# One PSUM tile for the early pairs and the dense layer, two dense tiles begun early, and q/k transposed by DMA from group 9

## The chip, the cores and the metric

The kernel runs on one core of one Trainium2 chip. The metric is the device time in microseconds (us) of one execution; the lower the better. A profiled execution of each kernel gives a trace, from which all durations below are taken.

## What is computed

Attention at two scales feeds a dense layer. For q, k, v of shape 8 x 8 x 576 x 64 (batch, heads, positions, width) the reference does, in essence:

```python
q_d = q.reshape(B, H, Sd, 4, D).mean(axis=3)      # k_d, v_d likewise
out_up = np.repeat(sm_attn(q_d, k_d, v_d), 4, axis=2)
mask = np.abs(pos[:, None] - pos[None, :]) < 4
scores = np.where(mask, scale * q @ k.T, -1e9)     # local attention
x = out_up + softmax(scores) @ v                    # then (4608, 512)
h = x @ w_in                                        # (4608, 2048)
out = (h - np.tanh(h)) @ w_out                      # (4608, 512)
```

## The kernel before, in words

**Attention.** The work is cut into 32 pairs of heads, and two pairs form one of 16 groups. Per group, q and k are loaded (`load_qk`), sorted into bf16 (`reorder`, line 491), transposed so that the width lies on the partitions (`turn`: nine TensorE transposes into PSUM, line 520, and a copy out, line 529; from group FI on, a DMA transpose on the SyncE queue instead, line 511, and a copy from SBUF), and summed over four positions (lines 533, 538). Per pair, `attention` makes the scores (lines 587, 606), their exponentials on ScalarE (623, 649, 652), a mask on VectorE (627, 656), the products with v (669, 675), the normalisation on VectorE (686, 688), and a transposition back into `xT`: by TensorE for pairs under 12 (lines 723/728 with a copy at 734, or 744 to 748), by a DMA transpose for the others (`lnT`, line 698) with two VectorE adds (line 708).

**Dense layer.** `dense(kb)` runs over nine blocks of 512 positions. `mm1` (line 777) makes one of 16 tiles of h with four matmuls of 128 x 512; ScalarE takes the tanh out of PSUM into `u` (line 786); VectorE subtracts it from the same PSUM bank into `gT` (line 789). `mm2` (line 832) makes one of four output tiles from 16 such matmuls; ScalarE copies it to `y` (line 843), and a DMA stores it. The last output tile is cut in three (`last_tile`, line 807). From block 2 on, `mm1` of one block and `mm2` of the block before alternate, so one pass through four `mm1` tiles and one output tile is 32 matmuls.

**PSUM.** [...] `ps_ts` and `ps_ox` hold two each for the attention. The other four are first `ps_ts1` and `ps_ox1`, two two-bank tiles for pairs 0 and 2, and then, once a pool is closed and another opened (`dense_banks`), four tiles of one bank each, `ps_hy0` to `ps_hy3`, which the dense tiles take in turn.

**Order.** `Program` collects operations with their engine, an assumed cost, and the keys that they read and write; `order` lays them out in time by priority, and `emit` issues every engine's instructions in that order. Where several engines may do an operation, tables (`RE`, `TU`, `TS`, `AS`, `AD`, `CV`, `UP`, `VD`, `RS`) say which. `spare` adds slack behind an operation before its user may be laid. `filler` puts matmuls on `warm` into idle places of TensorE until the first dense tile. The keys of `Program` decide the order alone. [...]

Of the kernel before, what the change touches and what calls it, by code (L numbers as in the profile page):

```python
# [8 lines left out]
FP32 = mybir.dt.float32  # L9
BF16 = mybir.dt.bfloat16  # L10
AF = mybir.ActivationFunctionType
ALU = mybir.AluOpType
PSUM = bass.MemoryType.PSUM


class Program:
# [20 lines left out]
    def op(self, eng, ns, fn, reads=(), writes=(), pri=0):  # L37
        i = len(self.ops)
        deps = set()
        for key in reads:  # L40
            if key in self.last_write:
                deps.add(self.last_write[key])
        for key in writes:
            if key in self.last_write:
                deps.add(self.last_write[key])
            deps.update(self.readers.get(key, ()))
        for key in reads:
            self.readers.setdefault(key, set()).add(i)
        for key in writes:
            self.last_write[key] = i  # L50
            self.readers[key] = set()
        deps.discard(i)
        self.ops.append((eng, ns, fn, deps, pri))
        self.touch.append(set(reads) | set(writes))
        return i
# [108 lines left out]
def kernel(  # L164
# [26 lines left out]
    N_DC = Dm // 128  # L191
# [4 lines left out]
    psum = ctx.enter_context(tc.tile_pool(name="psum", bufs=1, space=PSUM))  # L196

    def fixed(name, shape, dt, n=None, pool=const):
        if n is None:
            return pool.tile(shape, dt, name=name, tag=name)  # L200
        return [pool.tile(shape, dt, name=f"{name}{i}", tag=f"{name}{i}")
                for i in range(n)]
# [17 lines left out]
    vd = fixed("vd", [128, 2, 4, 65], BF16, NVW)  # L220
# [7 lines left out]
    lnT = fixed("lnT", [128, 7, 128], BF16, NLN)  # L228
    od = fixed("od", [128, G], BF16, 2)
# [6 lines left out]

    ps_ts = fixed("ps_ts", [128, 2, 512], FP32, pool=psum)
    ps_ox = fixed("ps_ox", [128, 2, 512], FP32, pool=psum)
    ps_hy = []


    early = ExitStack()
    psum_e = early.enter_context(tc.tile_pool(name="psum_e", bufs=1, space=PSUM))
    ps_ts1 = fixed("ps_ts1", [128, 2, 512], FP32, pool=psum_e)
    ps_ox1 = fixed("ps_ox1", [128, 2, 512], FP32, pool=psum_e)

    def dense_banks():
        early.close()
        pool = ctx.enter_context(tc.tile_pool(name="psum_d", bufs=1, space=PSUM))
        ps_hy.extend(fixed("ps_hy", [128, 512], FP32, 4, pool=pool))  # L250

    P = Program()

    def spare(pri, eng, to):
        if eng == "DMA":
            return 2500 if pri >= 140 else 1500 if pri >= 80 else 0
        level = (pri >= 120) + (pri >= LATER)
        return SPARE[to == "PE"].get(eng, (0, 0, 0))[level]
    LATER = 180
    SPARE = ({"POOL": (0, 500, 1000)},  # L260
             {"POOL": (0, 1000, 1500), "DVE": (0, 300, 800), "ACT": (0, 200, 500)})
    P.spare = spare
# [301 lines left out]
    def attention(p):  # L564
# [132 lines left out]
        if p >= XOUT:  # L697
            op("SP", 450, lambda: nc.sync.dma_start_transpose(
                out=lnT[sl], in_=ln[sl].rearrange("p n c -> p (n c)")),
               reads=[("ln", sl)], writes=[("lnT", sl), ("q", ("lnT", sl)), ("fl", p)],  # L700
               pri=pri - 60)
            op("DMA", T_OUT, None, reads=[("q", ("lnT", sl)), ("ln", sl)],
               writes=[("lnT", sl)], pri=pri)
            for t0, nt, n, up in ((0, 4, 120, lnT[sl][:, 5, 0:120]),
                                  (4, 1, 96, lnT[sl][:, 6, 104:128])):
                g = n // 4
                P.choice([(name, ns[t0 > 0], lambda eng=eng, t0=t0, nt=nt, n=n, g=g,
                           up=up: eng.tensor_tensor(  # L708
                    out=xo[:, QW * t0:QW * t0 + nt * n].rearrange(
                        "p (t g a) -> p t g a", t=nt, a=4),  # L710
                    in0=lnT[sl][:, t0:t0 + nt, 0:n].rearrange(
                        "p t (g a) -> p t g a", a=4),
                    in1=up[:, 0:nt * g].rearrange("p (t g) -> p t g", g=g).unsqueeze(3)
                    .to_broadcast([128, nt, g, 4]), op=ALU.add))
                          for name, ns, eng in XADD],
                         reads=[("lnT", sl)], writes=[("x", b, j)], pri=pri)
            return


# [44 lines left out]
    def mm1(kb, fc):  # L764
        slot, us, g = hy[0] % 4, un[0] % 3, kb % 2
        hy[0] += 1
        un[0] += 1
        bs = sorted({kb * 512 // S, (kb * 512 + 511) // S})

        cut = 3 if kb == 0 and fc < 4 else 2  # L770
        old = ["ts1", "ox1"] if kb == 0 and fc < 4 else []

        def mm(part):
            if not ps_hy:
                dense_banks()
            for dc in range(cut) if part == 0 else range(cut, N_DC):
                T.matmul(ps_hy[slot], w_in_sb[:, dc, fc * 128:(fc + 1) * 128],  # L777
                         xT[dc][:, kb * 512:kb * 512 + 512],
                         start=(dc == 0), stop=(dc == N_DC - 1))
        for part in range(2):  # L780
            dcs = range(cut) if part == 0 else range(cut, N_DC)
            op("PE", 216 * len(dcs), lambda part=part: mm(part),
               reads=[("w_in", fc // 4, c) for c in dcs] +
               [(name, b, j) for b in bs for j in dcs for name in ("x", "xh")],
               writes=[("hy", slot)] + old, pri=P_A if old and part == 0 else 5000)
        op("ACT", 490, lambda: A.activation(  # L786
            out=u[us], in_=ps_hy[slot], func=AF.Tanh),
           reads=[("hy", slot)], writes=[("u", us)], pri=-1)
        op("DVE", 620, lambda: V.tensor_tensor(  # L789
            out=gT[g][:, fc, :], in0=ps_hy[slot], in1=u[us], op=ALU.subtract),  # L790
           reads=[("hy", slot), ("u", us)], writes=[("gT", g, fc)], pri=-1)
# [59 lines left out]
    def dense(kb):  # L851
# [18 lines left out]
        if kb == NBLK:  # L870
# [2 lines left out]

    M2_FIRST = 16
    XOUT, T_OUT, AHEAD = 12, 1600, 7
    P_A, LATE = 5000, {0: 25, 2: 40, 3: 40}
    MERGE, GV = 14, 7
    FI, T_IN = 11, 2050
    XADD = [("DVE", (800, 350), V)]
    ORDER, W_FIRST = '0g123', '0123qv'  # L880
    TB = {(1, 0), (1, 1), (2, 0), (2, 1), (3, 0), (5, 0)}
    PV = {2: 0, 3: 0, 4: -1, 5: -1, 6: 0}
    PLACE = {2: (1, 3), 3: (1, 2), 4: (4, 4), 5: (1, 2), 6: (4, 4), 7: (1, 1), 8: (3, 3)}
    W_LATE = [0, 0, 0, 0]
    T_QK, T_V, T_W, W_PRI = 900, 780, 2750, 53
    CAST = [("POOL", 620, GP.tensor_copy), ("ACT", 620, A.copy),
# [1 line left out]
    CAST_V = [[("POOL", 790, GP.tensor_copy), ("ACT", 720, A.copy)],  # L888
              [("POOL", 790, GP.tensor_copy)], [("ACT", 720, A.copy)],
              [("DVE", 500, V.tensor_copy)]]  # L890
    CV = {0: 3, 1: 0, 2: 0, 3: 3, 4: 0, 5: 0, 6: 3, 7: 1, 8: 2, 9: 0, 10: 1, 11: 3}
    REORDER = [[("DVE", 860, V.tensor_copy), ("ACT", 950, A.copy),
                ("POOL", 1350, GP.tensor_copy)],
               [("DVE", 860, V.tensor_copy)], [("ACT", 950, A.copy)],
               [("DVE", 1150, V.tensor_copy)], [("POOL", 1350, GP.tensor_copy)]]
    RE = {(0, 0): 0, (0, 1): 0, (1, 0): 1, (1, 1): 1, (2, 0): 1, (2, 1): 0, (3, 0): 3, (3,
          1): 0, (4, 0): 2, (4, 1): 1, (5, 0): 0, (5, 1): 0}
    TURN = [[("ACT", 1125, A.copy), ("DVE", 1250, V.tensor_copy)],
            [("ACT", 1125, A.copy)], [("DVE", 1250, V.tensor_copy)],
            [("ACT", 2210, A.copy)]]  # L900
    TU = {(0, 0): 0, (0, 1): 0, (1, 0): 2, (1, 1): 2, (2, 0): 0, (2, 1): 0, (3, 0): 2, (3,
          1): 0, (4, 0): 0, (4, 1): 1, (5, 0): 1, (5, 1): 0}
    re_v, re_a, re_p = (("DVE", 480, V.tensor_copy), ("ACT", 580, A.copy),
                        ("POOL", 720, GP.tensor_copy))
    REORDER_H = [[[re_v, re_a, re_p]] * 2, [[re_v], [re_a]], [[re_v], [re_p]],
                 [[re_a], [re_p]]]
    POOLED = [[("ACT", 600, A.copy), ("DVE", 650, V.tensor_copy)],
              [("ACT", 600, A.copy)], [("DVE", 650, V.tensor_copy)]]
    PV1 = True
    VD = {0: 1, 1: 2, 2: 1, 3: 0, 4: 1, 5: 0, 6: 1}  # L910
    RS = {(0, 1): 2, (1, 0): 4, (1, 1): 1}
    UP = {0: 0, 1: 0, 2: 0, 3: 3, 4: 3, 8: 0, 11: 3}
    UP_COPY = [("ACT", 660, A.copy), ("DVE", 720, V.tensor_copy)]
    UP_H = [[("ACT", 370, A.copy)], [("DVE", 410, V.tensor_copy)]]
    half_v, half_p = ("DVE", 420, 260, V), ("POOL", 650, 500, GP)
# [2 lines left out]
              [[("DVE", 700, V.tensor_copy)], [("ACT", 640, A.copy)]]]  # L918
    ADD_H = [[[half_v, half_p]] * 2, [[half_v], [half_p]], [[half_v], [half_v]],
             [[half_p], [half_p]]]  # L920
    TS = {(0, 0): 1, (0, 1): 2, (1, 1): 2, (2, 1): 2, (4, 0): 2, (5, 0): 2, (5, 1): 1}
    AS = {(1, 0): 2, (1, 1): 1, (2, 0): 1, (2, 1): 1, (5, 0): 1, (5, 1): 4, (6, 1): 1}
    URG = {'e1': {4: -2, 5: -2, 6: -2, 7: -2, 8: -2, 9: -2, 10: -2, 11: -2}, 'e2': {0: -2,
          1: -2, 2: -2, 3: -2, 4: -2, 5: -2, 6: -2, 7: -2, 8: -2, 9: -2, 10: -2, 11: -2},
          'norm': {0: -2, 1: -2, 2: -2, 3: -2, 4: -2, 5: -2, 6: -2, 7: -2}, 'add': {0: -2,
          1: -2}, 'turn': {4: -2, 5: -2}, 'vd': {4: -2, 5: -2}}
    ADDERS = [[("DVE", 760, 440, V), ("POOL", 1190, 850, GP)],
              [("POOL", 1190, 880, GP)], [("DVE", 760, 440, V)]]
    AD = {(0, 0): 1, (0, 1): 0, (1, 0): 0, (1, 1): 1, (2, 0): 1, (2, 1): 0, (3, 0): 0, (3,
          1): 1, (4, 0): 0, (4, 1): 0, (5, 0): 0, (5, 1): 2}  # L930

    op("DVE", 180, lambda: V.memset(warm, 0.0), writes=["warm"], pri=-999)
    op("POOL", 500, c_ident, writes=["ident"], pri=-99)
# [162 lines left out]
```

The softmax here doesn't subtract the row's maximum and nothing guards it: scores larger than these inputs give would overflow.

## Time and profile before

| | |
|---|---|
| time, median of 3 | 334.98 us (334.89 to 335.55) |
| profiled span | 333.9 us |
| TensorE busy | 319.9 us, 96% |
| VectorE, ScalarE, GpSimd busy | 236.0, 209.6, 154.2 us |
| granted TensorE clock | 1.000 |
| chain that ended last | TensorE 83%, of that line 832 35% and line 777 34% of the span |

In the profile, PE is TensorE, PEld its weight loads, DVE VectorE, ACT ScalarE, POOL GpSimd and SP SyncE. A group of instructions is one line, with engine, operation, tiles and shapes; its two time columns are the busy time with the mean of one, and the idle time of that engine ahead of it with what ended it. A matmul's duration overlaps the next one's, so a sum of means is more than the busy time.

### The profile page before, as it was taken

What the parts mean: (1) busy time and instruction counts of PE and PEld (TensorE: products, weight loads), DVE (VectorE), ACT (ScalarE), POOL (GpSimd) and SP (SyncE); (2) the same over time, 40 slices, a digit from 0 to 9 for tenths busy, and PEclk for the clock granted to TensorE, in tenths of its full rate; (3) what the DMA queues carried; (4) which work ended last, traced back from release to release, by engine and by line L of the source; (5) the groups of instructions that cost most, each with busy time, mean ns of one, the idle gap of its engine ahead of it and who ended that gap; (6) DMA issues with size and microseconds to landing.
All of it is one profiled execution on the core that took longest, in us unless ns stands there. A gap on an engine that the chain in (4) does not pass through costs nothing.

```text
span 333.9 us, 6822 instructions
## 1 busy us (share of the span) xinstructions
PE 319.9 (96%) x2563; PEld 168.2 (50%) x2606; DVE 236.0 (71%) x386; ACT 209.6 (63%) x338; POOL 154.2 (46%) x183
## 2 busy tenths in 40 slices
PE   8778999999989999999999999999999999999996
PEld 5454555655554555554444444444444444444444
DVE  3697989789998898899687878787666443343300
ACT  1775877769948678668878786976654444444411
POOL 8673766248789477794929385652000000000000
PEclk9999999999999999999999999999999999999999
DMA  6999999999982779998999889843233000100012
GB/s 208 261 389 305 322 326 287 242 273 251 311 258 72 214 191 273 242 248 221 226 257 253 210 239 204 152 97 90 59 75 73 33 31 31 63 33 31 31 69 91
DMA packets 96878, 60.47 MB, mean 181 GB/s; under 512 B 74510, under 2 KB 80078, under 8 KB 96846
## 3 DMA queue, kind: packets, MB, share of 16 engines
q1 hardware_dynamic: 96846, 60.04, 67.2%
q8 instruction: 20, 0.33, 0.4%
q14 instruction: 12, 0.10, 0.1%
HBM read 43.05 MB, written 9.44 MB: 157 GB/s over the span
## 4 chain that ended last, share of the span: by engine, by line
PE 83%; DVE 9%; POOL 3%; issue 3%; ACT 1%; POOLq 0%; DVEq 0%; ACTq 0%
PE ps_hy L832 35%; PE ps_hy L777 34%; PE ps_ox L669 3%; PE ps_ts L587 3%; PE ps_ox L675 2%; DVE gT L789 2%; DVE ln L688 2%; PE ps_ts L520 2%; PE ps_hy L807 1%; DVE E L656 1%; DVE qk L529 1%; DVE half L533 1%; ACT qk L529 1%; DVE E L627 1%; PE ps_ox L606 1%
## 5 line engine op out<-in xcount | busy, mean ns | idle before, releaser
L777 PE MATMUL ps_hy<-xT,w_in_sb 128*128 128x512 bf16 x553 | 142.1, 379 | 2.3 <-issue 1.1
L832 PE MATMUL ps_hy<-w_out_sb,gT 128*128 128x512 bf16 x540 | 137.2, 379 | 1.4 <-issue 0.5
L789 DVE TENSOR_TENSOR gT<-ps_hy,uy 128x512 bf16<-128x512 f32 x144 | 95.1, 684 | 57.9 <-ACT uy L786 56.3
L786 ACT ACTIVATE uy<-ps_hy 128x512 f32<-128x512 f32 x144 | 83.6, 601 | 61.7 <-PE ps_hy L777 57.2
L777 PEld LDWEIGHTS <-w_in_sb 128*128 128x128 bf16 x576 | 53.1, 98 | 59.8 <-issue 1.7
L832 PEld LDWEIGHTS <-gT 128*128 128x128 bf16 x560 | 52.3, 98 | 58.1
L533 POOL TENSOR_TENSOR half<-qk 128x576 f32<-128x576 bf16 (+1 forms) x33 | 35.4, 1074 | 44.2 <-ACT qk L529 38.2
L688 DVE TENSOR_TENSOR ln<-ps_ox,r 128x896 bf16<-128x896 f32 x30 | 32.7, 1089 | 0.8
L623 ACT ACTIVATE E<-ps_ts 128x960 bf16<-128x960 f32 x30 | 29.4, 979 | 2.1 <-PE ps_ts L587 2.1
L843 ACT COPY uy<-ps_hy 128x512 f32<-128x512 f32 x35 | 20.6, 590 | 14.0 <-PE ps_hy L832 12.4
L443 POOL CAST vw<-vst 128x640 bf16<-128x640 f32 x27 | 23.6, 878 | 9.3 <-DMA vst<-in_v_dram 4.3
L627 DVE TENSOR_TENSOR E<-E,mask 128x960 bf16<-128x960 bf16 x28 | 24.4, 872 | 4.0 <-ACT E L623 3.8
L356 POOL TENSOR_TENSOR qkn<-qkn 128x512 f32<-128x512 f32 (+1 forms) x18 | 25.4, 1409 | 3.1 <-PE ps_ox L606 1.3
L529 ACT COPY qk<-ps_ts 128x1152 bf16<-128x1152 bf16 (+1 forms) x16 | 16.1, 1007 | 16.2 <-DVE qk L529 6.3
L708 DVE TENSOR_TENSOR xT<-lnT 128x480 bf16<-128x480 bf16 (+1 forms) x40 | 26.1, 668 | 0.0
L529 ACT COPY qk<-vst 128x1152 bf16<-128x1152 bf16 x10 | 22.1, 2207 | 1.2 <-POOL half L533 1.2
L538 POOL TENSOR_TENSOR qkd<-half 128x288 bf16<-128x288 f32 (+1 forms) x31 | 20.5, 664 | 5.0 <-DVE half L533 3.7
L491 DVE CAST qr<-qkn 128x1152 bf16<-128x1152 f32 (+1 forms) x18 | 17.8, 987 | 2.6 <-DMA qkn<-in_q_dram 2.2
L669 PEld LDWEIGHTS <-E 128*128 128x128 bf16 x300 | 15.2, 98 | 7.2 <-issue 0.8
L587 PEld LDWEIGHTS <-qk 64*128 64x128 bf16 x320 | 9.5, 95 | 17.8 <-issue 15.6
L669 PE MATMUL ps_ox<-vw,E 128*128 128x65 bf16 x300 | 18.0, 194 | 0.3 <-DVE xT L734 0.3
L491 POOL CAST qr<-qkn 128x1152 bf16<-128x1152 f32 (+1 forms) x14 | 15.8, 1129 | 5.1 <-DMA qkn<-in_k_dram 3.0
(107 smaller groups left out, 295.8 us busy)
## 6 DMA issues: line engine op xcount, KB each, us to landing
vst<-in_v_dram SPq DMA_DIRECT2D x62, 160.0 KB, 5.0
qkn<-in_q_dram SPq DMA_DIRECT2D x32, 288.0 KB, 4.2
qkn<-in_k_dram SPq DMA_DIRECT2D x32, 288.0 KB, 5.0
out_dram<-uy SPq DMA_DIRECT2D x35, 256.0 KB, 2.4
qkn<-in_v_dram SPq DMA_DIRECT2D x9, 512.0 KB, 5.1
gT<-in_moe_w_in_dram SPq DMA_DIRECT2D x4, 1024.0 KB, 8.8
xT<-in_moe_w_out_dram SPq DMA_DIRECT2D x8, 256.0 KB, 4.9
gT<-in_moe_w_out_dram SPq DMA_DIRECT2D x2, 1024.0 KB, 9.0
```

The lines of the kernel that those rows point to most:

```text
L491: P.choice([(eng, ns, lambda fn=fn, x0=x0, x1=x1: fn(out=dst[:, x0:x1], in_=srt[:, x0:x1])) for eng, ns, fn in table], reads=[("qkn", sn, ...
L529: fn(out=o[:, ys].rearrange("p y (g a) -> p y g a", a=A6), in_=b16.rearrange("p (a g y) -> p y g a", a=A6, y=2)[:, ys])
L533: eng.tensor_tensor(out=half[:, ys], in0=four[:, ys, :, 0:2], in1=four[:, ys, :, 2:4], op=ALU.add)
L623: op("ACT", 980, lambda: A.activation(out=e1, in_=ps[:, :, 0:480], func=AF.Exp, scale=SCALE), reads=ts, writes=[("E", se, 0)], pri=URG.get ...
L627: op("DVE", 900, lambda: V.tensor_tensor(out=e1, in0=e1, in1=mask[:, 0:480].unsqueeze(1).to_broadcast([128, 2, 480]), op=ALU.mult), reads= ...
L669: T.matmul(po[:, hh, 65 * t:65 * t + 65], E[se][:, c:c + 128], vw[w][:, 2 * jj + hh, t, :], start=True, stop=True)
L688: op("DVE", 1090, lambda: V.tensor_tensor(out=ln[sl].rearrange("p n (h d) -> p h n d", d=D), in0=blocks[:, :, :, 0:64], in1=r[s].unsqueeze ...
L708: up=up: eng.tensor_tensor(out=xo[:, QW * t0:QW * t0 + nt * n].rearrange("p (t g a) -> p t g a", t=nt, a=4), in0=lnT[sl][:, t0:t0 + nt, 0: ...
L777: T.matmul(ps_hy[slot], w_in_sb[:, dc, fc * 128:(fc + 1) * 128], xT[dc][:, kb * 512:kb * 512 + 512], start=(dc == 0), stop=(dc == N_DC - 1))
L786: op("ACT", 490, lambda: A.activation(out=u[us], in_=ps_hy[slot], func=AF.Tanh), reads=[("hy", slot)], writes=[("u", us)], pri=-1)
L789: op("DVE", 620, lambda: V.tensor_tensor(out=gT[g][:, fc, :], in0=ps_hy[slot], in1=u[us], op=ALU.subtract), reads=[("hy", slot), ("u", us) ...
L832: T.matmul(ps_hy[slot], gT[g][:, fc, ts * 128:ts * 128 + 128], w_out_sb[:, fc, :], start=(fc == 0), stop=(fc == N_FF - 1))
```

## The change

It has these parts:

- **PSUM.** `ps_ts1`, `ps_ox1` and the four dense tiles become views of one tile `ps_e` of four banks that lives for the whole kernel; the closing and opening of pools goes. Dense tiles 0 and 1 take the banks of `ps_ox1` and tiles 2 and 3 those of `ps_ts1`.
- **Early dense tiles.** Tiles 0 and 1 of block 0 are cut into two, one and one matmuls and claim only `ox1`, so that their first two matmuls can start when pairs 0 and 1 are done; tiles 2 and 3 claim `ts1`.
- **Slack.** Behind a DMA that VectorE uses directly (the transposes back) the planner leaves 1.0 us in place of 1.5 or 2.5; loads keep theirs. The line-708 adds become plain operations in place of choices with one entry, so that the rule sees them. `LATER` is 200 for 180.
- **q and k by DMA.** `FI` goes from 11 to 9: groups 9 and 10 are transposed by DMA too.
- **MERGE** is 13 for 14: the scores of pairs from 13 on share a step with the next pair's.
- **Tables.** Which engine does what is set anew, `LATE`, `PLACE`, `URG` and `PV1` too; `UP` gains pair 6.

```diff
-    ps_hy = []
-    early = ExitStack()
-    psum_e = early.enter_context(tc.tile_pool(name="psum_e", bufs=1, space=PSUM))
-    ps_ts1 = fixed("ps_ts1", [128, 2, 512], FP32, pool=psum_e)
-    ps_ox1 = fixed("ps_ox1", [128, 2, 512], FP32, pool=psum_e)
-    def dense_banks():
-        early.close()
-        pool = ctx.enter_context(tc.tile_pool(name="psum_d", bufs=1, space=PSUM))
-        ps_hy.extend(fixed("ps_hy", [128, 512], FP32, 4, pool=pool))
+    ps_e = fixed("ps_e", [128, 4, 512], FP32, pool=psum)
+    ps_ts1, ps_ox1 = ps_e[:, 0:2], ps_e[:, 2:4]
+    ps_hy = [ps_e[:, 2], ps_e[:, 3], ps_e[:, 0], ps_e[:, 1]]
...
     def spare(pri, eng, to):
+        if eng == "DMA" and to == "DVE":
+            return NEAR if pri >= 80 else 0
         if eng == "DMA":
             return 2500 if pri >= 140 else 1500 if pri >= 80 else 0
...
-    LATER = 180
+    LATER = 200
+    NEAR = 1000
...
-        cut = 3 if kb == 0 and fc < 4 else 2
-        old = ["ts1", "ox1"] if kb == 0 and fc < 4 else []
+        old, parts = [], (range(0, 2), range(2, 4))
+        if kb == 0 and fc < 4:
+            old = ["ox1"] if fc < 2 else ["ts1"]
+            parts = (range(0, 2), range(2, 3), range(3, 4)) if fc < 2 else (range(3), range(3, 4))
...
-    P_A, LATE = 5000, {0: 25, 2: 40, 3: 40}
-    MERGE, GV = 14, 7
-    FI, T_IN = 11, 2050
-    XADD = [("DVE", (800, 350), V)]
+    P_A, LATE = 5000, {1: 25, 2: 25}
+    MERGE, GV = 13, 7
+    FI, T_IN = 9, 2050
...
-    PV1 = True
+    PV1 = False
...
-    UP = {0: 0, 1: 0, 2: 0, 3: 3, 4: 3, 8: 0, 11: 3}
+    UP = {0: 2, 1: 0, 2: 1, 3: 3, 4: 2, 6: 3, 8: 0, 11: 3}
```

More of the change, by code (lines that the diff above doesn't have):

```diff
@@ L706, in attention @@
                 g = n // 4
-                P.choice([(name, ns[t0 > 0], lambda eng=eng, t0=t0, nt=nt, n=n, g=g,
-                           up=up: eng.tensor_tensor(
+                op("DVE", (800, 350)[t0 > 0], lambda t0=t0, nt=nt, n=n, g=g, up=up: V.tensor_tensor(
                     out=xo[:, QW * t0:QW * t0 + nt * n].rearrange(
@@ L713, in attention @@
                     in1=up[:, 0:nt * g].rearrange("p (t g) -> p t g", g=g).unsqueeze(3)
-                    .to_broadcast([128, nt, g, 4]), op=ALU.add))
-                          for name, ns, eng in XADD],
-                         reads=[("lnT", sl)], writes=[("x", b, j)], pri=pri)
+                    .to_broadcast([128, nt, g, 4]), op=ALU.add),
+                   reads=[("lnT", sl)], writes=[("x", b, j)], pri=pri)
             return
@@ L768, in mm1, with mm @@
         bs = sorted({kb * 512 // S, (kb * 512 + 511) // S})
-        cut = 3 if kb == 0 and fc < 4 else 2
-        old = ["ts1", "ox1"] if kb == 0 and fc < 4 else []
[L773 to L776, printed above, removed]
+        old, parts = [], (range(0, 2), range(2, 4))
+        if kb == 0 and fc < 4:
+            old = ["ox1"] if fc < 2 else ["ts1"]
+            parts = (range(0, 2), range(2, 3), range(3, 4)) if fc < 2 else (range(3), range(3, 4))
+        def mm(dcs):
+            for dc in dcs:
                 T.matmul(ps_hy[slot], w_in_sb[:, dc, fc * 128:(fc + 1) * 128],
@@ L779, in mm @@
                          start=(dc == 0), stop=(dc == N_DC - 1))
-        for part in range(2):
-            dcs = range(cut) if part == 0 else range(cut, N_DC)
-            op("PE", 216 * len(dcs), lambda part=part: mm(part),
+        for dcs in parts:
+            op("PE", 216 * len(dcs), lambda dcs=dcs: mm(dcs),
                reads=[("w_in", fc // 4, c) for c in dcs] +
                [(name, b, j) for b in bs for j in dcs for name in ("x", "xh")],
-               writes=[("hy", slot)] + old, pri=P_A if old and part == 0 else 5000)
+               writes=[("hy", slot)] + old, pri=P_A if old and dcs[-1] < 3 else 5000)
         op("ACT", 490, lambda: A.activation(
@@ L875 @@
     XOUT, T_OUT, AHEAD = 12, 1600, 7
-    P_A, LATE = 5000, {0: 25, 2: 40, 3: 40}
-    MERGE, GV = 14, 7
-    FI, T_IN = 11, 2050
-    XADD = [("DVE", (800, 350), V)]
+    P_A, LATE = 5000, {1: 25, 2: 25}
+    MERGE, GV = 13, 7
+    FI, T_IN = 9, 2050
     ORDER, W_FIRST = '0g123', '0123qv'
-    TB = {(1, 0), (1, 1), (2, 0), (2, 1), (3, 0), (5, 0)}
+    TB = {(1, 0), (1, 1), (2, 0), (2, 1), (3, 0)}
     PV = {2: 0, 3: 0, 4: -1, 5: -1, 6: 0}
-    PLACE = {2: (1, 3), 3: (1, 2), 4: (4, 4), 5: (1, 2), 6: (4, 4), 7: (1, 1), 8: (3, 3)}
+    PLACE = {2: (0, 0), 3: (1, 2), 4: (4, 4), 5: (1, 2), 6: (4, 4), 7: (1, 1), 8: (2, 2)}
     W_LATE = [0, 0, 0, 0]
@@ L890 @@
               [("DVE", 500, V.tensor_copy)]]
-    CV = {0: 3, 1: 0, 2: 0, 3: 3, 4: 0, 5: 0, 6: 3, 7: 1, 8: 2, 9: 0, 10: 1, 11: 3}
+    CV = {0: 3, 1: 1, 2: 2, 3: 3, 4: 0, 5: 1, 6: 3, 7: 1, 8: 2, 9: 0, 10: 0, 11: 3}
     REORDER = [[("DVE", 860, V.tensor_copy), ("ACT", 950, A.copy),
@@ L895 @@
                [("DVE", 1150, V.tensor_copy)], [("POOL", 1350, GP.tensor_copy)]]
-    RE = {(0, 0): 0, (0, 1): 0, (1, 0): 1, (1, 1): 1, (2, 0): 1, (2, 1): 0, (3, 0): 3, (3,
-          1): 0, (4, 0): 2, (4, 1): 1, (5, 0): 0, (5, 1): 0}
+    RE = {(0, 0): 0, (0, 1): 1, (1, 0): 4, (1, 1): 2, (2, 0): 1, (2, 1): 0, (3, 0): 4, (3,
+          1): 0, (4, 0): 2, (4, 1): 4, (5, 0): 0, (5, 1): 1}
     TURN = [[("ACT", 1125, A.copy), ("DVE", 1250, V.tensor_copy)],
@@ L900 @@
             [("ACT", 2210, A.copy)]]
-    TU = {(0, 0): 0, (0, 1): 0, (1, 0): 2, (1, 1): 2, (2, 0): 0, (2, 1): 0, (3, 0): 2, (3,
-          1): 0, (4, 0): 0, (4, 1): 1, (5, 0): 1, (5, 1): 0}
+    TU = {(0, 0): 0, (0, 1): 1, (1, 0): 0, (1, 1): 2, (2, 0): 0, (2, 1): 2, (3, 0): 0, (3,
+          1): 0, (4, 0): 0, (4, 1): 2, (5, 0): 2, (5, 1): 0}
     re_v, re_a, re_p = (("DVE", 480, V.tensor_copy), ("ACT", 580, A.copy),
@@ L908 @@
               [("ACT", 600, A.copy)], [("DVE", 650, V.tensor_copy)]]
-    PV1 = True
-    VD = {0: 1, 1: 2, 2: 1, 3: 0, 4: 1, 5: 0, 6: 1}
-    RS = {(0, 1): 2, (1, 0): 4, (1, 1): 1}
-    UP = {0: 0, 1: 0, 2: 0, 3: 3, 4: 3, 8: 0, 11: 3}
+    PV1 = False
+    VD = {0: 2, 1: 1, 2: 1, 3: 0, 4: 0, 5: 2, 6: 1}
+    RS = {(0, 1): 2, (1, 1): 3, (2, 1): 1, (3, 0): 4}
+    UP = {0: 2, 1: 0, 2: 1, 3: 3, 4: 2, 6: 3, 8: 0, 11: 3}
     UP_COPY = [("ACT", 660, A.copy), ("DVE", 720, V.tensor_copy)]
@@ L920 @@
              [[half_p], [half_p]]]
[L921 to L926, printed above, removed]
+    TS = {(0, 0): 3, (0, 1): 1, (1, 1): 1, (2, 1): 1, (4, 0): 1, (4, 1): 3, (5, 0): 3, (5,
+          1): 2, (6, 1): 1}
+    AS = {(0, 0): 1, (1, 0): 1, (1, 1): 1, (2, 0): 1, (2, 1): 2, (3, 0): 4, (5, 0): 4, (5,
+          1): 4, (6, 1): 2}
+    URG = {'e1': {0: -2, 1: -2}, 'e2': {0: -2, 1: -2, 2: -2, 3: -2, 4: -2, 5: -2, 6: -2, 7:
+          -2, 8: -2, 9: -2, 10: -2, 11: -2}, 'od': {0: -2, 1: -2, 2: -2, 3: -2, 4: -2, 5:
+          -2, 6: -2, 7: -2}, 'norm': {8: -2, 9: -2, 10: -2, 11: -2}, 'add': {0: -2, 1: -2},
+          'turn': {4: -2, 5: -2}, 'vd': {4: -2, 5: -2}}
     ADDERS = [[("DVE", 760, 440, V), ("POOL", 1190, 850, GP)],
               [("POOL", 1190, 880, GP)], [("DVE", 760, 440, V)]]
-    AD = {(0, 0): 1, (0, 1): 0, (1, 0): 0, (1, 1): 1, (2, 0): 1, (2, 1): 0, (3, 0): 0, (3,
-          1): 1, (4, 0): 0, (4, 1): 0, (5, 0): 0, (5, 1): 2}
+    AD = {(0, 0): 0, (0, 1): 2, (1, 0): 0, (1, 1): 1, (2, 0): 0, (2, 1): 0, (3, 0): 2, (3,
+          1): 1, (4, 0): 1, (4, 1): 0, (5, 0): 2, (5, 1): 0}
     op("DVE", 180, lambda: V.memset(warm, 0.0), writes=["warm"], pri=-999)
```

## The prediction

> **What bounds the kernel now.** I read the page first: the header, the engines, the costliest groups.
>
> ```profile
> span 333.9 us, 6822 instructions
> PE 319.9 (96%) x2563; PEld 168.2 (50%) x2606; DVE 236.0 (71%) x386; ACT 209.6 (63%) x338; POOL 154.2 (46%) x183
> ...
> PE 83%; DVE 9%; POOL 3%; issue 3%; ACT 1%; POOLq 0%; DVEq 0%; ACTq 0%
> ...
> L777 PE MATMUL ps_hy<-xT,w_in_sb 128*128 128x512 bf16 x553 | 142.1, 379 | 2.3 <-issue 1.1
> L832 PE MATMUL ps_hy<-w_out_sb,gT 128*128 128x512 bf16 x540 | 137.2, 379 | 1.4 <-issue 0.5
> L789 DVE TENSOR_TENSOR gT<-ps_hy,uy 128x512 bf16<-128x512 f32 x144 | 95.1, 684 | 57.9 <-ACT uy L786 56.3
> L786 ACT ACTIVATE uy<-ps_hy 128x512 f32<-128x512 f32 x144 | 83.6, 601 | 61.7 <-PE ps_hy L777 57.2
> L843 ACT COPY uy<-ps_hy 128x512 f32<-128x512 f32 x35 | 20.6, 590 | 14.0 <-PE ps_hy L832 12.4
> ```
>
> TensorE is the bound, and the two dense groups lose under 4 us in waits. The tanh, the subtraction and the copy cost 0.60, 0.68 and 0.59 us each, 144, 144 and 35 times, and none shows on the path: TensorE works in another bank meanwhile. The timeline of the last stage shows this:
>
> ```profile
> 297.03 1.89 PE L777 MATMUL ps_hy<-xT,w_in_sb 128*128 128x512 bf16 x8
> 298.52 1.09 ACT L786 ACTIVATE uy<-ps_hy 128x512 f32<-128x512 f32 x2 [1.57 <-PE ps_hy L777]
> ...
> 298.75 1.03 PE L832 MATMUL ps_hy<-w_out_sb,gT 128*128 128x512 bf16 x4
> 299.15 1.29 DVE L789 TENSOR_TENSOR gT<-ps_hy,uy 128x512 bf16<-128x512 f32 x2 [2.33 <-ACT uy L786]
> ...
> 299.62 1.03 PE L777 MATMUL ps_hy<-xT,w_in_sb 128*128 128x512 bf16 x4
> ```
>
> From 297.03 to the record at 303.93 stand 32 matmuls: 6.90 us, 0.216 each. One lasts 0.379, so 0.16 us drains after a group before anyone can read. Last, the chain of waits where the dense work starts:
>
> ```profile
> 28.85 0.41 ACT xT L734
> 29.26 0.02 issue
> 29.29 0.47 DVE xT L734
> 29.75 0.04 issue
> 29.80 4.69 PE ps_hy L777 x21
> ```
>
> Pair 3's result lies in the two banks of `ps_ts`. ScalarE copies bank 0, VectorE bank 1, into different halves of `xT`, and yet VectorE starts only when ScalarE is done. So two accesses to one PSUM tile wait for each other even in different banks. A handover costs 0.02 to 0.05 us.
>
> [...]
>
> **The change: the wait that it adds.** `ps_hy0..3` were four tiles; now they are four banks of one tile, `ps_e`. If one tile means one queue of accesses, as at 29.26, every dense matmul waits for each reader of any bank that was issued before it, and each reader for all matmuls issued before it. The program built from the changed source says just that. Its issue order late in the kernel (line numbers of before):
>
> ```
> PE  L777 x2 -> bank 3, L832 x2 -> bank 2
> ACT L786 tanh of bank 3     (waits for the L832 just above)
> PE  L832 x2 -> bank 2       (the first waits for that tanh)
> PE  L777 x2 -> bank 0
> DVE L789 reads bank 3       (waits for the L777 just above)
> PE  L777 x2 -> bank 0       (the first waits for that L789)
> ```
>
> In before, no L832 waits for a tanh; now some 80 do. A pause is therefore 0.16 drain + 0.02 to the reader + the reader + 0.05 back: 0.83 us for a tanh, 0.91 for a subtraction, 0.82 for a copy. Two readers in one place also wait for each other: 1.53. Behind the waiting matmul stand all of TensorE's later instructions, attention included; behind those, the exponentials and normalisations.
>
> I counted the places in the built order where a dense matmul follows at least one reader of `ps_e`: 263. In 206 TensorE has nothing between:
>
> - 90 tanh alone x 0.83 = 74.7
> - 75 subtractions alone x 0.91 = 68.3
> - 12 copies alone x 0.82 = 9.8
> - 14 subtraction and copy, 13 tanh and subtraction, x 1.53 = 41.3
> - 2 in the last tile, 1.3
>
> That is 195.4. In the other 57 (single to four readers, 72.7 us by the same prices) attention matmuls stand between and run meanwhile: a pair's products 0.55 us, its scores 0.7 to 0.8, nine transposes 0.50. They take 33.3 off: 39.4. **Together +235.** A check on the last stage: per 32 matmuls four tanh, three subtractions and one double place, 3.3 + 2.7 + 1.5 = 7.5 us on 6.9, so 14.4. The attention's own ScalarE and VectorE work does not add: walked from the products of one pair to those of the next, 52 matmuls with readers come to about 26 us, and exponentials, masks, normalisation and the 2.2-us copies of L529 end inside TensorE's bursts. I take 0, up to 35 for the range.
>
> **Start.** Pairs 0 and 2 use `ps_e` too. Pair 0's small exponentials now follow pair 2's copy out of the other half (L529, 1.35 us), and pair 0's products follow pair 2's scores and exponential. Walking the start with the durations of before, the first matmul that needs pair 3 moves from 29.80 to about 32.8, with six dense matmuls behind it and not three: 3.0 - 0.65 = **+2.4**. So the early tiles gain their 0.65 us and lose it to the shared tile.
>
> **Removed.** 36 TensorE transposes of groups 9 and 10; nine take from 36.55 to 37.06 before the next work, 0.50: 4 x 0.50 = **-2.0**. The extra `UP` pair costs 0.1. Their place takes a DMA transpose (4.2 us to landing, issued well ahead) and a ScalarE copy of 2.21 us for one of about 1.0: +4.8 us on an engine 63% busy, hidden by the dense matmuls. The adds after `lnT` (3.1 us to landing) are planned at least 0.5 us nearer; L708 idles 0.0 in before, and the pauses widen every distance, so 0. `MERGE`, tables, `LATE`: regrouped work, hidden under the pauses, 0.
>
> 335 + 235 + 2.4 - 2.0 = 570.
>
> **Rivals.**
>
> 1. *The clock drops* (0.10). [...] For it: [...]half-busy stretches that long are not in this trace. Against: no pause exceeds 3 us, and from 10 to 20 us TensorE, with gaps, kept 1.00. A quarter of the 1136 dense matmuls at half speed adds 284 x 0.21 = 60: 630.
> 2. *Half the pauses are hidden* (0.05), readers being ahead of the matmuls named: 335 + 118 = 453. Against: readers name the last matmul issued.
> 3. *No pause at all* (0.03): every semaphore is already there when TensorE arrives, as in before, where waits of L777 and L832 sum to under 4 us. Then 335 - 2.0 - 0.65 = 332, faster. Against it, a tanh cannot be done before the matmul that it waits for.
>
> **Numbers.** Main case 0.82, 570. Per-pause error of 0.05 us is 13 us over 263, and queueing gives up to 35: 545 to 615 holds most of it. The clock case is partly outside, rivals 2 and 3 wholly. Slower 0.96, same 0.01, faster 0.03.
>
> **What would show it.** TensorE's share near 55 to 60%; L777 and L832 with about 200 us idle ahead, ended by ACT L786, DVE L789 and ACT L843 (at their new lines); 14.4 us per 32 matmuls after the last pair; the chain of waits passing through tanh and subtraction; L520 36 fewer. If tanh records overlap matmuls on other banks of `ps_e`, the prediction is wrong at its root; if the clock row falls under 9, rival 1.

## The result, and the profile after

| | before | after |
|---|---|---|
| time, median | 335.00 us (334.89 to 335.55) | 658.82 us (651.17 to 663.91) |
| profiled span | 333.9 us | 658.6 us |
| TensorE busy | 319.9 us | 438.5 us |
| TensorE idle (span less busy) | 14.0 us | 220.1 us |
| granted TensorE clock | 1.000 | 0.818 |

The changed kernel takes 1.958 times as long, with a 95% interval of 1.941 to 1.976. The slowest of its four runs, 663.91 us, is over 1.5% above the fastest and counts as slow; the factor is of the other three. The forecast was 570 us, with a range of 545 to 615.

The page of the changed kernel: header, busy times, TensorE and its clock in 40 slices (tenths), the chain by engine, and the dense groups (busy time, mean ns of one, idle time ahead and what ended most of it).

```profile
span 658.6 us, 6866 instructions
...
PE 438.5 (67%) x2564; PEld 187.8 (29%) x2564; DVE 231.5 (35%) x387; ACT 220.3 (33%) x341; POOL 146.2 (22%) x185
...
PE   8656797557767656667666766665666576656676
...
PEclk9966799999697999966898588999768855686659
...
PE 59%; DVE 17%; ACT 17%; issue 5%; POOL 0%; DVEq 0%; ACTq 0%; POOLq 0%
...
L769 PE MATMUL ps_e<-xT,w_in_sb 128*128 128x512 bf16 x576 | 197.1, 462 | 97.1 <-DVE gT L780 61.6
L823 PE MATMUL ps_e<-w_out_sb,gT 128*128 128x512 bf16 x560 | 186.7, 445 | 109.0 <-ACT uy L777 59.2
L780 DVE TENSOR_TENSOR gT<-ps_e,uy 128x512 bf16<-128x512 f32 x144 | 99.0, 691 | 376.2 <-PE ps_e L769 171.6
L777 ACT ACTIVATE uy<-ps_e 128x512 f32<-128x512 f32 x144 | 85.4, 597 | 325.0 <-PE ps_e L823 174.5
...
L834 ACT COPY uy<-ps_e 128x512 f32<-128x512 f32 x35 | 20.5, 585 | 62.3 <-DVE gT L780 29.9
```

The readers of the dense banks last what they lasted before (691, 597 and 585 ns against 684, 601 and 590). What is new stands in three places. The idle time ahead of the two dense groups is 97.1 and 109.0 us instead of 2.3 and 1.4. The chain holds 17% VectorE and 17% ScalarE, against 9% and 1%. And the mean dense matmul lasts 462 and 445 ns instead of 379 and 379, and the clock row is under 9 in 23 of its 40 slices, down to 5.

What TensorE waited for (sum in us, times, longest):

```profile
PE ps_e L769 <- DVE gT L780: 61.6, 73, 2.3
PE ps_e L823 <- ACT uy L777: 59.2, 78, 1.5
PE ps_e L823 <- DVE gT L780: 29.4, 31, 2.3
PE ps_e L769 <- ACT uy L777: 28.7, 38, 1.7
PE ps_e L823 <- ACT uy L834: 20.0, 18, 1.5
PE ps_e L769 <- ACT uy L834: 6.4, 8, 1.5
```

They are 205.3 us in 246 waits. L823, the second dense product, has no use for a tanh of the bank that L777 reads, and yet waits for it 78 times. So accesses to different banks of `ps_e` took turns: the waits of this program went by the tile that an instruction names and not by the bank (59.2 us in those 78). The longest single wait is 2.3 us. The timeline of the last stage (start, duration, what, and in brackets the engine's idle time before it and what ended it) shows the pauses, and in its second half something more:

```profile
562.91 0.59 PE L823 MATMUL ps_e<-w_out_sb,gT 128*128 128x512 bf16 x2 [0.74 <-ACT uy L777]
...
563.60 0.60 ACT L777 ACTIVATE uy<-ps_e 128x512 f32<-128x512 f32 x1 [0.74 <-PE ps_e L823]
564.25 0.59 PE L823 MATMUL ps_e<-w_out_sb,gT 128*128 128x512 bf16 x2 [0.74 <-ACT uy L777]
...
564.95 0.69 DVE L780 TENSOR_TENSOR gT<-ps_e,uy 128x512 bf16<-128x512 f32 x1 [7.47 <-PE ps_e L823]
565.69 1.01 PE L769 MATMUL ps_e<-xT,w_in_sb 128*128 128x512 bf16 x2 [0.85 <-DVE gT L780]
```

TensorE, the tanh and the subtraction work strictly in turn, no two of them side by side. Two matmuls that took 0.59 us at 562.91 take 1.01 us from 565.69 on: the clock has halved (the trace has it at 0.50 from 565.03 on), in the middle of pauses of 0.74 to 0.85 us. In stretches of the changed kernel's run (length; busy us and instructions of TensorE, weight loads, VectorE, ScalarE, GpSimd; clock; DMA share; GB/s):

```profile
100.00:150.00 50.00, 32.36 (x295) 17.39 (x295) 28.75 (x46) 24.37 (x44) 22.03 (x27) 1.00 0.38 107
500.00:550.00 50.00, 30.95 (x88) 10.19 (x87) 7.61 (x11) 8.32 (x14) 0.00 (x0) 0.74 0.04 16
600.00:640.00 40.00, 26.88 (x63) 8.28 (x63) 5.53 (x8) 5.46 (x10) 0.00 (x0) 0.57 0.04 13
```

**Where the 325 us come from.** The span grew by 324.7 us: TensorE's idle time by 206.1 and its busy time by 118.6. The idle time is the waits above. Of the busy time, about 40 us is, by the author's estimate, the drain that ends each group before a reader starts, which overlapped the next matmul before: 246 to 263 pauses of 0.16 us each, the 0.379 us of one matmul less the 0.216 from one start to the next. About 76 us is the clock: 360 of the 1136 dense matmuls (204 of L769, 156 of L823) start while the trace has the clock at 0.50, and each is 0.21 us longer (half of 1.01 - 0.59). They last 612 and 617 ns in the mean and the others 379, which together gives the 462 and 445 of the page. That leaves some 3 us; 177 other matmuls, most of them of the attention, ran at half clock too.

The time of a run also goes with its mean clock: 651.17 us at 0.841, 657.35 at 0.833, 660.29 at 0.818 and 663.91 at 0.811.

### The profile page after: what moved, and what is told of

It reads as the page before. It is cut to its first block, busy times and chain, and to the rows that moved or that the text cites. A ratio compares the mean times of both kernels' runs of the same rounds, so it can differ in the third digit from the quotient of the medians.

```text
span 658.6 us, 6866 instructions
## 1 busy us (share of the span) xinstructions
PE 438.5 (67%) x2564; PEld 187.8 (29%) x2564; DVE 231.5 (35%) x387; ACT 220.3 (33%) x341; POOL 146.2 (22%) x185
## 4 chain that ended last, share of the span: by engine, by line
PE 59%; DVE 17%; ACT 17%; issue 5%; POOL 0%; DVEq 0%; ACTq 0%; POOLq 0%
PE ps_e L769 28%; PE ps_e L823 26%; DVE gT L780 15%; ACT uy L777 13%; ACT uy L834 3%; PE ps_ts L1056 1%; PE ps_ox L663 1%; DVE qk L523 1%; DVE ln L682 1%; PE ps_e L798 1%; ACT qk L523 1%; PE ps_ox L669 1%; PE ps_ts L581 0%; PE ps_ox L456 0%; POOL half L527 0%
## 5 line engine op out<-in xcount | busy, mean ns | idle before, releaser
L769 PE MATMUL ps_e<-xT,w_in_sb 128*128 128x512 bf16 x576 | 197.1, 462 | 97.1 <-DVE gT L780 61.6
L823 PE MATMUL ps_e<-w_out_sb,gT 128*128 128x512 bf16 x560 | 186.7, 445 | 109.0 <-ACT uy L777 59.2
L780 DVE TENSOR_TENSOR gT<-ps_e,uy 128x512 bf16<-128x512 f32 x144 | 99.0, 691 | 376.2 <-PE ps_e L769 171.6
L777 ACT ACTIVATE uy<-ps_e 128x512 f32<-128x512 f32 x144 | 85.4, 597 | 325.0 <-PE ps_e L823 174.5
L823 PEld LDWEIGHTS <-gT 128*128 128x128 bf16 x560 | 59.5, 109 | 215.2 <-issue 184.8
L769 PEld LDWEIGHTS <-w_in_sb 128*128 128x128 bf16 x576 | 62.7, 110 | 201.0 <-issue 166.2
L834 ACT COPY uy<-ps_e 128x512 f32<-128x512 f32 x35 | 20.5, 585 | 62.3 <-DVE gT L780 29.9
L523 ACT COPY qk<-vst 128x1152 bf16<-128x1152 bf16 x14 | 30.4, 2171 | 0.0
L669 PE MATMUL ps_ox<-vd,E 128*128 128x65 bf16 x232 | 17.3, 200 | 0.0
L581 PE MATMUL ps_ts<-qk 64*128 64x120 bf16 x262 | 14.9, 227 | 0.7 <-ACT qk L523 0.7
```

The source lines that it names most:

```text
L523: fn(out=o[:, ys].rearrange("p y (g a) -> p y g a", a=A6), in_=b16.rearrange("p (a g y) -> p y g a", a=A6, y=2)[:, ys])
L581: T.matmul(to[:, c:c + NQ[t]], qT[rows, k0:k0 + 128], qT[rows, QW * t:QW * t + NQ[t]], start=not first, stop=not first or t > 2)
L777: op("ACT", 490, lambda: A.activation(out=u[us], in_=ps_hy[slot], func=AF.Tanh), reads=[("hy", slot)], writes=[("u", us)], pri=-1)
L780: op("DVE", 620, lambda: V.tensor_tensor(out=gT[g][:, fc, :], in0=ps_hy[slot], in1=u[us], op=ALU.subtract), reads=[("hy", slot), ("u", us) ...
L823: T.matmul(ps_hy[slot], gT[g][:, fc, ts * 128:ts * 128 + 128], w_out_sb[:, fc, :], start=(fc == 0), stop=(fc == N_FF - 1))
L834: op("ACT", 490, lambda: A.copy(out=y[ys], in_=ps_hy[slot]), reads=[("hy", slot)], writes=[("y", ys)], pri=-1)
```

## The experiments

Two theories stood at the start. A: the one tile `ps_e` makes all users of its four banks take turns, and TensorE, left half empty, then also loses its clock. B: the change's other parts (tables, slack, the start, q/k by DMA) carry a good part of the loss. Three more questions followed: whether the clock falls because TensorE is too empty, how empty is too empty, and what the rest of the change is worth.

**The shared tile alone.** Before, with nothing changed but the tile:

```diff
-    psum_e = early.enter_context(tc.tile_pool(name="psum_e", bufs=1, space=PSUM))
-    ps_ts1 = fixed("ps_ts1", [128, 2, 512], FP32, pool=psum_e)
-    ps_ox1 = fixed("ps_ox1", [128, 2, 512], FP32, pool=psum_e)
...
+    ps_e = fixed("ps_e", [128, 4, 512], FP32, pool=psum)
+    ps_ts1, ps_ox1 = ps_e[:, 0:2], ps_e[:, 2:4]
+    ps_hy = [ps_e[:, 2], ps_e[:, 3], ps_e[:, 0], ps_e[:, 1]]
...
-            if not ps_hy:
-                dense_banks()
```

> The kernel before with one edit: the four dense banks and the two early tiles are views of one tile of four banks; order, tables, DMA use as before. Theory (the shared tile is the whole cause): the same lockstep as in the changed kernel, some 250 pauses worth 230 us, plus what the clock loses, so 630 to 670 us, L832 ended by ACT L786, clock near 0.82. Rival (the new tables, the two more groups by DMA or the nearer adds are the cause): within 10 us of 335.

It took 665.53 us in its one run, at a clock of 0.814, and lies in the expected band. TensorE's largest waits in it:

```profile
PE ps_e L766 <- DVE gT L778: 68.4, 77, 1.7
PE ps_e L821 <- ACT uy L775: 53.0, 69, 1.5
PE ps_e L766 <- ACT uy L775: 29.2, 42, 2.0
```

These are the waits of the changed kernel, with nothing else of the change present; TensorE's order of issue is that of the kernel before. With the two next rows, 27.5 and 26.2 us, they come to 204.3 us against 205.3. The shared tile is enough for the whole loss, and B falls.

**One tile, two tiles.** The changed kernel, with `ps_e` as two tiles of two banks:

```diff
-    ps_e = fixed("ps_e", [128, 4, 512], FP32, pool=psum)
-    ps_ts1, ps_ox1 = ps_e[:, 0:2], ps_e[:, 2:4]
-    ps_hy = [ps_e[:, 2], ps_e[:, 3], ps_e[:, 0], ps_e[:, 1]]
+    ps_ts1 = fixed("ps_ts1", [128, 2, 512], FP32, pool=psum)
+    ps_ox1 = fixed("ps_ox1", [128, 2, 512], FP32, pool=psum)
+    ps_hy = [ps_ox1[:, 0], ps_ox1[:, 1], ps_ts1[:, 0], ps_ts1[:, 1]]
```

> The changed kernel with two tiles of two banks in place of one of four: dense tiles 0 and 1 lie in ps_ox1, 2 and 3 in ps_ts1; order and early start as in the change. Theory (a matmul waits for readers of any bank of its own tile and of no other): the waits become fewer, about 107 places left with 62 us of pauses, so 395 to 420 us, with the clock above 0.9. Rival (the waits come from the early claims and the order, not from what shares a tile): near 650.

It took 407.94 us in its one run, within the expected band. Of its page, TensorE's busy time and the clock row:

```profile
PE 334.3 (82%) x2521; PEld 167.0 (41%) x2564; DVE 230.2 (57%) x387; ACT 217.3 (53%) x341; POOL 151.0 (37%) x185
...
PEclk9999999999999999999999999999999999999999
```

TensorE's idle time is 71.9 us (406.2 - 334.3) against 220.1 with four banks in a tile. The order of issue and the banks are the same; only what counts as one tile differs. With TensorE 82% busy the clock stays at 0.999. So this run parts the two losses: two banks to a tile cost pauses and no clock.

**The pauses filled.** In the changed kernel, five matmuls of 320 columns on `ps_ts` ahead of each dense matmul that follows a reader of `ps_e`, per reader, after the attention's last operation only. Their results are not used.

```diff
...
+            if any(key[0] == "hy" for key in self.touch[i] if isinstance(key, tuple)):
+                if self.ops[i][0] != "PE":
+                    readers += 1
+                else:
+                    if readers and n > last:
+                        filler("ts", 5 * readers)
+                    readers = 0
...
```

> The changed kernel with more work: after the last attention operation, five idle matmuls of 128x320 on the free tile ps_ts (0.68 us at full clock) stand ahead of each dense matmul that follows a reader of the shared tile, so TensorE is busy inside its pauses. Their result is used by nobody. Theory (TensorE's clock falls because TensorE stands still half the time): the clock is 1.00 over the last stage, dense matmuls there are 0.216 us apart, and that stage, 197 us from the last pair's products to the end, takes 79.6 us as in before plus about 68 us of pauses, so 150; in all 605 to 620 us, less than the changed kernel although more is done. Rival (the clock falls for another reason, such as time or heat): clock of the stage still near 0.68, and the time 658 or more.

It took 623.06 us (620.7 to 624.11), 1.859 times the kernel before (1.855 to 1.862). That is some 35 us less than the changed kernel, although TensorE does more, and 3 us above the expected band. The same stretch as above, and TensorE's records across two tanh waits (L1065 is the filling):

```profile
500.00:550.00 50.00, 47.14 (x251) 24.66 (x254) 9.34 (x14) 9.52 (x16) 0.00 (x0) 1.00 0.04 16
```

```profile
541.40 0.59 PE L832 MATMUL ps_e<-w_out_sb,gT 128*128 128x512 bf16 x2
541.83 0.84 PE L1065 MATMUL ps_ts<-warm 128*128 128x320 bf16 x5
542.74 0.59 PE L832 MATMUL ps_e<-w_out_sb,gT 128*128 128x512 bf16 x2
```

The clock is 1.00 where the changed kernel had 0.74. The wait for the tanh is still there, with work in it: from one pair of L832 to the next it is 542.74 - 541.40 = 1.34 us, as in the changed kernel (564.25 - 562.91). From the last product of the attention to the end it takes 157 us (461.8 to 619.0) against 197 (461.6 to 658.6). In that stage 195 of the changed kernel's dense matmuls ran at half clock, which at 0.21 us each is 41 us; 40 came back. Before 460 us, where nothing was filled, both run alike.

**How full is enough.** The same with two instead of five:

```diff
-                        filler("ts", 5 * readers)
+                        filler("ts", 2 * readers)
```

> The filled kernel with two instead of five unused matmuls of 320 columns per reader, again only after the attention's last operation, about 197 us in the changed kernel. The waits stay as they are. Work on TensorE in that stretch: 32 dense matmuls 6.9 us and 9 readers x 2 x about 0.14 = 2.6 us per 14.4 us, 66%, against 48% in the changed kernel and 90% or more with five. If the clock depends on how full TensorE is and two thirds is enough, the windows from 470 us on show 0.95 to 1.00 and the time is again about 620. If every pause of about 0.5 us counts, the clock there stays at 0.6 to 0.8 as in the changed kernel and the time is 645 to 660. In between, the clock is a matter of degree.

It took 625.41 us in its one run. The stretch, and a few of TensorE's records in it:

```profile
500.00:550.00 50.00, 35.15 (x166) 15.94 (x165) 9.29 (x14) 10.11 (x17) 0.00 (x0) 1.00 0.04 16
```

```profile
520.77 0.59 PE L832 MATMUL ps_e<-w_out_sb,gT 128*128 128x512 bf16 x2
521.21 0.43 PE L1065 MATMUL ps_ts<-warm 128*128 128x320 bf16 x2
522.10 0.59 PE L832 MATMUL ps_e<-w_out_sb,gT 128*128 128x512 bf16 x2 [0.46 <-ACT uy L786]
```

The pauses that are left, 0.4 to 0.6 us each and 0.9 behind a copy, do not lower the clock, which is 1.00 here. TensorE is busy 0.87 of 1.33 us here, 65%; in the changed kernel, across the same tanh pause (562.91 to 564.25), 0.59 of 1.34, 44%, and the clock halved just after. So for the clock a pause that is half filled was as good here as one filled to the end (1.00 from 500 to 550 us with two and with five). How busy TensorE was before the clock changed is read from the changed kernel's trace in the last section.

**Four tiles, with the start of before.** The changed kernel with the pools, `dense_banks` and the cut of block 0's tiles taken back to before:

```diff
-        old, parts = [], (range(0, 2), range(2, 4))
-        if kb == 0 and fc < 4:
-            old = ["ox1"] if fc < 2 else ["ts1"]
...
+        cut = 3 if kb == 0 and fc < 4 else 2
+        old = ["ts1", "ox1"] if kb == 0 and fc < 4 else []
```

> The changed kernel with the PSUM part undone: the pools and four one-bank tiles of before, and before's start of the first four dense tiles (three matmuls, then one, claiming both early tiles). Tables, slack, MERGE and q/k by DMA from group 9 stay. Theory (the shared tile is the whole loss, the rest is worth the 36 transposes taken off TensorE): 332 to 334 us, clock 1.00. Rival (the rest costs something too): above 337.

It took 337.79 us, 1.0074 times before (1.0046 to 1.0102): 4 us above the expected band, as its rival had it, and 0.7% slower than before. The clock is 1.00 and its largest dense wait sums to 1.3 us, so it confirms the tile once more, but the rest of the change does not bring 2 us with this start. The loss is not at the start alone: between 100 and 250 us TensorE is busy 146.3 us, against 148.0 in before. The altered claims also moved the planner's order: TensorE's differs from that of the changed kernel from the first dense matmuls on. Which of its steps costs the time is left open.

**Four tiles and the early start.** The whole change with its order of issue, but each two-bank tile in a pool of its own, closed and replaced by two one-bank tiles when the dense tile that claims it begins:

```diff
-    ps_e = fixed("ps_e", [128, 4, 512], FP32, pool=psum)
...
+    def dense_banks(slot):
+        n = slot // 2
+        (early_ox, early_ts)[n].close()
+        pool = ctx.enter_context(tc.tile_pool(name=f"psum_d{n}", bufs=1, space=PSUM, side=("right", "left")[n]))
+        ps_hy[2 * n:2 * n + 2] = [
+            pool.tile([128, 512], FP32, name=f"ps_hy{2 * n + i}", tag=f"ps_hy{2 * n + i}")
+            for i in range(2)]
...
+            if ps_hy[slot] is None:
+                dense_banks(slot)
```

> The whole change with the banks in tiles of their own: pair 0's tile is closed on its own and its place taken by dense tiles 0 and 1, later pair 2's by dense tiles 2 and 3, so that the early start stays and no two dense banks share a tile. Same order of issue as the change. Theory: no pauses, clock 1.00, and against the previous kernel 0.65 us less for the three dense matmuls begun earlier: 331.5 to 333.5 us. Rival (closing early tiles one by one brings waits of its own): 335 or more.

It took 333.77 us, 0.9941 times before (0.9922 to 0.9961): 0.3 us above the expected band, and the only kernel here that is clearly, if by 0.6%, below the one before. Its dense groups, and TensorE's records where the dense work starts:

```profile
L782 PE MATMUL ps_hy<-xT,w_in_sb 128*128 128x512 bf16 x553 | 142.5, 379 | 1.5 <-issue 0.5
L836 PE MATMUL ps_hy<-w_out_sb,gT 128*128 128x512 bf16 x541 | 138.3, 379 | 1.4 <-issue 0.3
```

```profile
29.25 0.59 PE L782 MATMUL ps_hy<-xT,w_in_sb 128*128 128x512 bf16 x2
...
30.60 7.34 PE L782 MATMUL ps_hy<-xT,w_in_sb 128*128 128x512 bf16 x31
```

The idle time ahead of the dense groups is 2.9 us again instead of 206.1, the matmul 379 ns, and TensorE's order of issue is that of the changed kernel from end to end. The early tiles begin in the banks that pair 0 leaves, as the change wants, without the shared tile.

**What its parts are worth.** The kernel of the experiment before, with `FI` back at 11:

```diff
-    FI, T_IN = 9, 2050
+    FI, T_IN = 11, 2050
```

> The previous kernel with q and k of groups 9 and 10 transposed by TensorE again (FI 11). Theory: four times nine transposes come back at 0.50 us each, so 2.0 us more than the previous kernel (1.5 to 2.5). Rival (the DMA transposes and the 2.2-us copies on ScalarE cost as much as they save): no difference, within 0.5 us.

It took 335.92 us, 1.0009 times before (0.9995 to 1.0023): the two groups by DMA bring 2.15 us, as expected. The planner moves other work along with such a setting, here and in the next run, so this is the worth of the setting as a whole. Without them the early start, the slack and the tables together bring nothing that can be told from zero. And the same kernel with the old slack, `FI` at 9:

```diff
-        if eng == "DMA" and to == "DVE":
-            return NEAR if pri >= 80 else 0
```

> The kernel of e5_four_tiles_early with the old slack of 1.5 and 2.5 us behind the DMA transposes back too (the two lines on DMA and VectorE taken out). Theory: the adds never waited for their DMA before, so their place matters little: within 0.7 us of e5_four_tiles_early. Rival (nearer adds let xT and so the dense tiles come earlier): 1 us or more slower.

It took 335.08 us, 0.9985 times before (0.9967 to 1.0002): 1.3 us more than with the new slack, where 0.7 at most was expected, so its rival came. The two intervals, up to 0.9961 and from 0.9967, just miss each other, so the slack seems to be worth something, but hardly more than these runs can tell.

## Why the prediction was wrong

The step that failed is the dismissal of rival 1: "Against: no pause exceeds 3 us, and from 10 to 20 us TensorE, with gaps, kept 1.00." The first half was true and did not help: no wait exceeded 2.3 us, and the clock fell to 0.57 to 0.74 in whole stretches. That only a pause longer than 3 us would cost the clock was the author's assumption; no trace showed it. The second half compared with the wrong stretch: from 10 to 20 us TensorE was busy 7.51 of 10 us, 75%, while the changed kernel's clock fell after stretches of 3.41 us in which it was busy 30 to 51% (last section). The step priced the clock at zero in the main case and gave it a chance of 0.10; it cost about 76 us, for 360 dense matmuls at half clock. With the pauses filled by unused work the clock after the attention returned to 1.00 and 40 us of that stage came back, though a matmul still waited as long for its reader. So it is shown that the emptiness costs the clock, and not the waits as such; before 460 us, where nothing was filled, the same cause is read from the trace alone.

A share of busy time can be too low with no long pause. In the changed kernel's trace the clock changed on a grid of 3.41 us, and it halved after pauses of 0.74 us at 44% busy; with two unused matmuls to a reader it stayed full with pauses of 0.46 us at 65%.

The other steps, in the order of the prediction:

- **One tile, one queue: right.** Waits of L823 on a tanh went from none to 78, and the tile alone gave 665.53 us. Accesses to different banks did overlap where the banks were tiles of their own: the same order of issue on one-bank tiles ran in 333.77 us, with 2.9 us of idle time ahead of the dense groups. What serialised the banks was the tile that the program named, not the memory.
- **263 pauses, +235: right in number, a little short in size.** Idle 205 us and drain of about 40 make 245. A tanh pause takes 564.25 - 562.91 - 0.43 for the two matmuls = 0.91 us, not 0.83: the reader starts 0.10 us after the modelled end of the matmuls and not 0.02, which was read where VectorE follows ScalarE. In the last stage a pass at full clock takes 15.2 us (from the run of eight matmuls at 502.41 to the next at 517.65), against 14.4, and one at half clock 20.6 (538.36 to 558.96).
- **Start, +2.4: right in kind, 1.3 by the same reckoning.** The first matmul that needs pair 3 starts at 31.71 and not at 32.8 (29.80 before), with six dense matmuls ahead of it as foretold:

```profile
29.08 0.60 PE L769 MATMUL ps_e<-xT,w_in_sb 128*128 128x512 bf16 x2
...
30.42 1.03 PE L769 MATMUL ps_e<-xT,w_in_sb 128*128 128x512 bf16 x4
31.71 0.81 PE L769 MATMUL ps_e<-xT,w_in_sb 128*128 128x512 bf16 x3 [0.26 <-DVE xT L726]
```

- **36 transposes, -2.0: right.** Taken back in the kernel without the pauses, they cost 2.15 us.
- **Slack, 0:** in a kernel without the pauses perhaps 1.3. In the changed kernel it can't be seen.
- **Early tiles, 0.65:** not settled. Taking the start back cost 4.0 us (333.77 to 337.79), but it changed the order far behind the start as well.
- **The other rivals:** neither half of the pauses nor all of them were hidden.

At a clock of 1.00 the pauses, the start and the transposes by their measured sizes would make 335 + 245 + 1.3 - 2.2 = 579 (the start as 31.71 - 29.80 less the 0.65 of the early tiles). The clock put about 76 us on top and 3 stay unplaced. What came was rival 1. Its own sum, 630, was short by the pauses' 10 and by 16 of the clock: it took a quarter of the dense matmuls at half speed, and 32% were.

## What to carry to other kernels

Before you join PSUM banks into one tile, count which instructions will now name the same tile: here the dense matmuls also waited for readers of three banks that they never touched, 246 waits and 205.3 us in all, and splitting the tile by pool, with the same order of issue, gave the early start without the waits. When a change leaves TensorE half empty, price its clock too, by the busy share over a few microseconds and not by the longest gap: here it halved after 20 windows of 3.41 us that were 30 to 51% busy, in a kernel whose longest wait was 2.3 us. And when a rival adds to the main case rather than replacing it, its cost belongs in the range.

## What was not expected of the hardware

TensorE's clock halved and came back within one pass of 15 to 20 us, in a stage where no wait exceeds 1.5 us. TensorE's records of the changed kernel over two such passes:

```profile
558.15 1.01 PE L823 MATMUL ps_e<-w_out_sb,gT 128*128 128x512 bf16 x2 [1.47 <-ACT uy L834]
558.96 3.21 PE L769 MATMUL ps_e<-xT,w_in_sb 128*128 128x512 bf16 x8
...
583.42 0.59 PE L823 MATMUL ps_e<-w_out_sb,gT 128*128 128x512 bf16 x2 [0.74 <-ACT uy L777]
584.76 0.59 PE L823 MATMUL ps_e<-w_out_sb,gT 128*128 128x512 bf16 x2 [0.74 <-ACT uy L777]
586.21 0.59 PE L769 MATMUL ps_e<-xT,w_in_sb 128*128 128x512 bf16 x2 [0.85 <-DVE gT L780]
```

It comes back in the run of eight matmuls without a pause, 3.21 us long (the pair before it at 558.15 takes 1.01 us, the one after it, shown further above at 562.91, 0.59), and falls after the two tanh pauses that follow. One pass later, from 583.42 on, the same sequence with the same pauses keeps the full clock.

The trace shows what goes with it. Until its end it has the clock in stretches of 3.41, 6.83, 13.65, 20.48 us and so on, every one a whole multiple of 3.41. Cut on this grid, the two passes look like this (window, length, TensorE's busy us and records, the other engines; then the clock):

```profile
558.21:561.62 3.41, 3.41 (x9) 1.18 (x9) 0.00 (x0) 0.00 (x0) 0.00 (x0) 0.50 0.21 77
561.62:565.03 3.41, 1.73 (x7) 0.53 (x6) 0.08 (x1) 1.19 (x2) 0.00 (x0) 1.00 0.00 0
565.03:568.45 3.42, 1.98 (x5) 0.65 (x5) 1.30 (x2) 0.00 (x0) 0.00 (x0) 0.50 0.00 0
...
582.10:585.51 3.41, 1.76 (x7) 0.56 (x6) 0.05 (x1) 1.19 (x2) 0.00 (x0) 1.00 0.00 0
585.51:588.93 3.42, 1.62 (x6) 0.58 (x6) 1.33 (x2) 0.24 (x1) 0.00 (x0) 1.00 0.02 5
...
592.34:595.75 3.41, 1.36 (x6) 0.57 (x6) 0.69 (x1) 1.11 (x2) 0.00 (x0) 1.00 0.00 0
595.75:599.17 3.42, 3.42 (x10) 1.22 (x8) 0.00 (x0) 0.00 (x0) 0.00 (x0) 0.50 0.21 77
```

In these two passes TensorE's busy share in one window goes with the clock of the next. The window busy throughout (3.41 us) is followed by 1.00, the one of 40% (1.36 us) by 0.50, and the two that part the passes are close together: 1.73 us was followed by 0.50 and 1.76 us by 1.00. Over the changed kernel's trace, the full clock fell after 20 windows, 30 to 51% busy, and stayed after 100 windows, 43 to 100% busy; the halved clock came back after 20 windows, 80 to 100% busy, and stayed halved after 50, 40 to 81% busy. So in this trace every fall came after a window at most 51% busy and every return after one at least 80% busy. Neither figure parts the windows sharply by this measure, in which the ends of matmuls are modelled: between 43 and 51% both outcomes occur (the 1.62 us above, 47%, were followed by 1.00), and so they do between 80 and 81%.

The length of a pause alone does not decide: with two banks to a tile single waits reached 1.2 us, TensorE was busy 78% of the time from 300 to 400 us (77.96 of 100), and the clock stayed at 0.999 in the mean of the run. Between 100 and 150 us the changed kernel kept 1.00 with no window under 51%. With two unused matmuls to a reader the stage from 500 to 600 us kept 1.00 with TensorE busy 70% of it (70.39 of 100): there, 120 records of them (0.43 us a pair) were enough, and the kernel took some 32 us less.
